# Decode attention over a K/V window: loading K and V one head at a time, or four heads at a time from one ring of buffers

## The chip, the cores and the metric

The kernel runs on one core of one Trainium2 chip. The metric is the device time of one execution in microseconds; lower is better. Engines are named as in the profile: PE is TensorE (matmuls), PEld its weight loads, ACT is ScalarE, DVE is VectorE, POOL is GpSimd, SP is SyncE, which issues nearly all DMAs (SPq is its queue).

## The reference

A decode step with one token for each of 8 sequences: layer norm, attention with 32 query heads and 8 K/V heads over the last 2048 cached positions, output projection and residual, then a small MLP block. The token-shift branch of that block is zero for one token, so only the following is left:

```python
B, D, Hq, Hkv, Sk, Dh, W = 8, 512, 32, 8, 8192, 128, 2048
q = (layernorm(x) @ wq)                          # [8, 32, 128]
k = k_cache[:, :, Sk - W:, :]                    # [8, 8, 2048, 128], each head serves 4 query heads
v = v_cache[:, :, Sk - W:, :]
p = softmax(q . k * Dh ** -0.5)                  # per sequence and query head, over 2048 positions
h = x + (p . v).reshape(8, 4096) @ wo
u = layernorm(h)
x1 = u
h2 = h + x1 + gelu(layernorm(x1) @ w3) @ w4      # w3 [512, 1792], w4 [1792, 512]
```

K and V of the window are 67.1 MB in bf16; wq and wo are 4.2 MB each, w3 and w4 1.8 MB each.

## The kernel before

**Prologue.** x is loaded and normalised, wq is loaded (32 KB per partition), and 128 matmuls (`pe_q`, L211) make q for all heads. `dve_q` puts the four queries of each K/V head at their place in `qblk`, a tile that POOL zeroed (L182), so that the 32 columns of one head's weights are zero except for its own four.

**Items.** The unit of work is one K/V head of one sequence (batch row): 64 items of 2048 positions. K of an item is one DMA of 512 KB into one of 11 slots of `knat`, 128 partitions with 16 positions (4 KB, one contiguous run) each. V is the same with 13 slots of `vnat`. For each item PE does:

- `pe_T` (L238): 16 transposes of 128x128 into PSUM, in two halves; `evict` copies the first half to SBUF on ACT (L246) and the second on DVE (L248).
- `pe_QK` (L256): four matmuls of 512 positions each in the four 32-column strips of the array. The eight items of a batch row accumulate into one score tile of 128x512: row 32q + h holds query head h over a quarter q of the positions.
- `pe_PV` (L313): 16 matmuls with V as weights and four columns of the transposed probabilities moving.

**Softmax of a batch row**, once for each eight items, is cut in five parts that lie between later items: the row maximum on DVE (`softmax_1`), its transpose and combination over the quarters (`softmax_2`), the negated maximum as a column and the exp of the whole 128x512 tile on ACT with its row sums (`softmax_3`, L282), four transposes of the probabilities and one copy to `pT_sb` (`softmax_4`, L291, L295), and the sum over the quarters and its reciprocal (`softmax_5`).

**Order.** One Python loop over steps p fixes the program order of every engine: in step p come the load of K for item p, its transposes and evictions, the softmax part that is due, QK for item p - 2 (`LQK`), and the load of V and PV for item p - 13 (`LV`). Each engine works through its own list in order and waits on semaphores; a wait holds back all that follows it in that list. SP's list has the loads in the order of the steps, wo in four parts at steps 15, 23, 31 and 39 (it reuses wq's buffer), and w3 and w4 at the end.

**End.** For the last batch row each head has its own PSUM area; after a head's PV comes its scaling by the reciprocal (`scale`) and the 16 matmuls of its four query heads with wo (`pe_wo`, L344). Then `hs` is copied (L409), and norm, w3, gelu, w4 and the store follow.

Of the kernel before, what the change touches and what calls it, by code (L numbers as in the profile page):

```python
# [6 lines left out]
dt = mybir.dt  # L7
# [4 lines left out]
B = 8  # L12
D = 512
H = 32
# [12 lines left out]
NK = 11  # L27
NV = 13
NKT = 4
LQK = 2  # L30
LV = 13
WO_AT = (15, 23, 31, 39)
# [32 lines left out]
def bass_sequential_preLN__sliding_block_cached__mixer_s_mlp__decode_kernel(  # L65
# [23 lines left out]
    with es:  # L89
# [27 lines left out]
        qblk = sb([128, B, G, H], dt.bfloat16, "qblk")  # L117
        knat = sb([128, NK, NC * DH], dt.bfloat16, "knat")
        vnat = sb([128, NV, NC * DH], dt.bfloat16, "vnat")
        kT_sb = sb([128, NKT, W], dt.bfloat16, "kT_sb")  # L120

        P_sb = sb([128, 2, 512], dt.bfloat16, "P_sb")
        pT_sb = sb([128, 2, NC, H], dt.bfloat16, "pT_sb")
# [27 lines left out]
        kT_ps = [ps_t([128, W], dt.bfloat16, f"kT_ps{i}") for i in range(2)]  # L151
# [9 lines left out]

        sem_k = [S(f"sem_k{i}") for i in range(NK)]
        sem_v = [S(f"sem_v{i}") for i in range(NV)]
# [4 lines left out]
        def dma(eng, dst, src, sem, *waits):  # L168
            def f(e):
# [12 lines left out]
        e_qz = PO.op(lambda e: e.memset(qblk[:], 0.0))  # L182
# [10 lines left out]
        e_sel = DV.op(lambda e: e.tensor_reduce(sel_f[:, :], ident_f[:, :].rearrange("p (q h) -> p h q", q=4),  # L193
                                                AX.X, ALU.add), e_idf)
# [11 lines left out]
        dma(SP, wq_v, A_wq.rearrange("(p k) n -> p k n", k=KC), sem_wq)  # L206

# [8 lines left out]
        def dve_q(e):  # L216
            for g in range(G):
                ins = e.tensor_scalar(qblk[:, :, g, R * g:R * (g + 1)],  # L218
                                      S_ps[0][:, R * g * B:R * (g + 1) * B].rearrange("p (i b) -> p b i", b=B),
                                      inv_sqrt_dh, None, ALU.mult)  # L220
            return ins
        e_qblk = DV.op(dve_q, e_q, e_qz)


        e_Tlo, e_Thi, e_lo, e_hi, e_QK, e_PV = {}, {}, {}, {}, {}, {}
        e_max, e_mT, e_neg, e_negps, e_negc, e_exp, e_PT, e_pT, e_lsel, e_Lb, e_rL, e_scale = ({} for _ in range(12))

        def K(i):
            return sem_k[i % NK], 16 * (i // NK + 1)

        def V(i):
            return sem_v[i % NV], 16 * (i // NV + 1)

        def pe_T(i):
            def half(lo):
                def f(e):
                    for c in range(lo, lo + NC // 2):
                        ins = e.matmul(kT_ps[i % 2][:, c * 128:(c + 1) * 128],  # L238
                                       knat[:, i % NK, c * DH:(c + 1) * DH], ident_b[:, :], is_transpose=True)
                    return ins  # L240
                return f
            e_Tlo[i] = PE.op(half(0), K(i), e_lo.get(i - 2), e_idb)
            e_Thi[i] = PE.op(half(NC // 2), e_hi.get(i - 2))

        def evict(i):
            e_lo[i] = AC.op(lambda e: e.activation(kT_sb[:, i % NKT, 0:W // 2], kT_ps[i % 2][:, 0:W // 2], ACT.Copy),  # L246
                            e_Tlo[i], e_QK.get(i - NKT))
            e_hi[i] = DV.op(lambda e: e.tensor_copy(kT_sb[:, i % NKT, W // 2:W], kT_ps[i % 2][:, W // 2:W]),  # L248
                            e_Thi[i], e_QK.get(i - NKT))

        def pe_QK(i):
            b, g = divmod(i, G)

            def f(e):
                for q in range(4):
                    ins = e.matmul(S_ps[b % 2][32 * q:32 * (q + 1), :], qblk[:, b, g, :],  # L256
                                   kT_sb[:, i % NKT, 512 * q:512 * (q + 1)],
                                   start=(g == 0), stop=(g == G - 1),
                                   tile_position=(0, 32 * q), skip_group_check=True)
                return ins  # L260
            e_QK[i] = PE.op(f, e_lo[i], e_hi[i], e_qblk, e_exp.get(b - 2))


        def softmax_1(b):
            e_max[b] = DV.op(lambda e: e.tensor_reduce(mcol[:, :], S_ps[b % 2][:, :], AX.X, ALU.max),  # L265
                             e_QK[G * b + G - 1], e_mT.get(b - 1))

        def softmax_2(b):
            e_mT[b] = PE.op(lambda e: e.matmul(sm[0:1, MROW], mcol[:, :], ident_f[:, :], start=True, stop=True),
                            e_max[b], e_rL.get(b - 1), e_idf)  # L270
            e = DV.op(lambda e: e.tensor_reduce(Mrow[:, :], sm[0:1, MROW].rearrange("o (q h) -> o h q", q=4),
                                                AX.X, ALU.max), e_mT[b])
            m_bc = bass.AP(tensor=Mrow[:, :].tensor, offset=0, ap=[[H, 1], [0, 4], [1, H]])
            e_neg[b] = DV.op(lambda e: e.tensor_scalar(negrow[:, :].rearrange("o (q h) -> o q h", q=4), m_bc,
                                                       -1.0, None, ALU.mult), e, e_negps.get(b - 1))

        def softmax_3(b):
# [4 lines left out]
            e_exp[b] = AC.op(lambda e: e.activation(P_sb[:, j, :], S_ps[j][:, :], ACT.Exp, bias=negcol[:, j:j + 1],  # L282
                                                    scale=1.0, accum_out=lcol[:, j:j + 1]),
                             e_negc[b], e_PT.get(b - 2), e_lsel.get(b - 2))

        def softmax_4(b):
            j = b % 2

            def f(e):
                for jt in range(4):  # L290
                    ins = e.matmul(pT_ps[:, jt * 128:(jt + 1) * 128], P_sb[:, j, 128 * jt:128 * (jt + 1)],  # L291
                                   ident_b[:, :], is_transpose=True)
                return ins
            e_PT[b] = PE.op(f, e_exp[b], e_negc[b])
            e_pT[b] = DV.op(lambda e: e.tensor_copy(  # L295
                pT_sb[:, j, :, :].rearrange("p (q jt) h -> p q jt h", jt=4),
                pT_ps[:, 0:NC * H].rearrange("p (jt q h) -> p q jt h", jt=4, q=4)),
                e_PT[b], e_PV.get(G * (b - 2) + G - 1))
            e_lsel[b] = DV.op(lambda e: e.tensor_scalar(lsel[:, :], sel_f[:, :], lcol[:, j:j + 1], None, ALU.mult),
                              e_Lb.get(b - 1), e_sel)  # L300

        def softmax_5(b):
            e_Lb[b] = PE.op(lambda e: e.matmul(sm[:, LB], ones_f[:, :], lsel[:, :], start=True, stop=True),
                            e_lsel[b], e_pT[b])
            e_rL[b] = DV.op(lambda e: e.reciprocal(rL[:, b % 2, :], sm[:, LB]), e_Lb[b],
                            e_scale.get(b - 2))

        def pe_PV(i, dst, *waits):
            b, g = divmod(i, G)

            def f(e):
                for c in range(NC):
                    ins = e.matmul(dst, vnat[:, i % NV, c * DH:(c + 1) * DH],  # L313
                                   pT_sb[:, b % 2, c, R * g:R * (g + 1)], start=(c == 0), stop=(c == NC - 1))
                return ins
            e_PV[i] = PE.op(f, V(i), e_pT[b], *waits)

        def scale(b, heads, src, *waits):
            return DV.op(lambda e: e.tensor_tensor(oT_all[:, heads, b], src, rL[:, b % 2, heads], ALU.mult),
                         e_rL[b], *waits)  # L320


        def load_k(i):
            dma(SP, knat[:, i % NK, :].rearrange("p (c d) -> p c d", c=NC),
                A_k_cache[i // G, i % G, W0:SK, :].rearrange("(p c) d -> p c d", c=NC), sem_k[i % NK],
                e_Thi.get(i - NK))

        def load_v(i):
            dma(SP, vnat[:, i % NV, :].rearrange("p (c d) -> p c d", c=NC),
                A_v_cache[i // G, i % G, W0:SK, :].rearrange("(p c) d -> p c d", c=NC), sem_v[i % NV],  # L330
                e_PV.get(i - NV))

        hT_ps = S_ps[0]
        e_sc7, e_wo = {}, []

        def pe_wo(g):
            def f(e):
                if g == 0:
# [3 lines left out]
                for h in range(R * g, R * (g + 1)):  # L342
# [4 lines left out]
            e_wo.append(PE.op(f, e_sc7[g], e_exp[NB - 2], e_scale[NB - 2], (sem_wo, 16 * len(WO_AT)), X))  # L347

        LAST = NB - 1
        E_LAST = G * LAST + G - 1 + LQK  # L350
        for p in range(NITEM + LV + 1):
            if p < NITEM:
                load_k(p)
                pe_T(p)
                evict(p)
            if p in WO_AT:
                n = WO_AT.index(p)
                hh = H // len(WO_AT)
                dma(SP, wo_v[:, n * hh:(n + 1) * hh, :],
                    A_wo[n * hh * DH:(n + 1) * hh * DH, :].rearrange("(h p) n -> p h n", p=DH), sem_wo, e_q)  # L360
            for b in range(NB):
                base = G * b + (G - 1) + LQK
# [4 lines left out]
                elif p == base + 3:  # L367
                    softmax_4(b)
                elif p == base + 4:
                    softmax_5(b)  # L370
            if 0 <= p - LQK < NITEM:
                pe_QK(p - LQK)
                b, g = divmod(p - LQK, G)
                if g == G - 1:
                    softmax_1(b)
            i = p - LV
            if 0 <= i < NITEM:
                load_v(i)
                b, g = divmod(i, G)
                heads = slice(R * g, R * (g + 1))  # L380
                if b < LAST:
                    pe_PV(i, oT_ps[:, heads], e_scale.get(b - 1))
                    if g == G - 1:
                        e_scale[b] = scale(b, slice(0, H), oT_ps[:, 0:H], e_PV[i])
                else:
                    dst = kbank[g % 4][:, 0:R]
                    pe_PV(i, dst, e_lo[NITEM - 1], e_hi[NITEM - 1], e_lo[NITEM - 2], e_hi[NITEM - 2],
                          e_sc7.get(g - 4))
                    e_sc7[g] = scale(b, heads, dst, e_PV[i])
# [125 lines left out]
```

## Time and profile before

| | us |
|---|---|
| median of 3 runs | 202.52 (202.40 to 202.85) |
| span of the profiled execution, first to last instruction | 200.5 |
| PE busy in it | 154.7 (77%) |
| ACT busy | 79.5 (40%) |
| DVE busy | 69.3 (35%) |
| K transposes on PE (L238), 1024 | 78.5 |
| K evictions on ACT (L246), 64 | 65.5 |
| exp on ACT (L282), 8 | 5.5 |
| DMA of the hardware queue | 79.18 MB, 97.7% of 16 engines' span |

The profile's times are from one execution's span, which leaves out what lies before the first and after the last instruction; the runs' times have that in them. Busy times of an engine are sums over stages that are limited by different things, and PE's clock varies (the mean granted clock was 0.839 of full speed), so the same matmul has more than one duration in the trace.

### The profile page before, as it was taken

To read this page: it belongs to the slowest core of one execution; us is meant where nothing else is said; L and a number is where in the kernel's file an instruction comes from. 1 tells how busy PE (TensorE), PEld (TensorE's weight loads), DVE (VectorE), ACT (ScalarE), POOL (GpSimd) and SP (SyncE) were. 2 spreads that over 40 slices of the span, in tenths; PEclk is the share of its full clock that TensorE was granted. 3 is DMA by queue.
4 is the path that set the end of the run, shared out by engine and by line. 5 is a ranking of instruction groups with operands and counts; after the bars stand their busy time and mean duration, and the time that the engine had idled before them with its cause. 6 is when DMAs were issued, how large, how long until landed. Compare 5 with 4: busy or idle time off the path is not lost.

```text
span 200.5 us, 6047 instructions
## 1 busy us (share of the span) xinstructions
PE 154.7 (77%) x2765; PEld 124.5 (62%) x2765; DVE 69.3 (35%) x165; ACT 79.5 (40%) x91; POOL 2.5 (1%) x10
## 2 busy tenths in 40 slices
PE   0039999798973998567883898878977869979685
PEld 0039777675862786356662776656765657669574
DVE  6103556434431344213341154324532343132122
ACT  6003778743541454423542255442644254240021
POOL 4000000000000000000000000000000000000000
PEclk9999999997999599958998599996999696555555
DMA  7989999999999999999999999999999999999950
GB/s 243 464 360 418 418 416 416 401 418 422 414 401 416 421 414 415 404 418 414 418 403 412 418 421 416 416 420 418 421 414 414 421 417 419 418 421 415 421 243 14
DMA packets 23641, 79.58 MB, mean 397 GB/s; under 512 B 2232, under 2 KB 6336, under 8 KB 23360
## 3 DMA queue, kind: packets, MB, share of 16 engines
q1 hardware_dynamic: 23600, 79.18, 97.7%
q8 instruction: 22, 0.36, 0.6%
q14 instruction: 3, 0.02, 0.0%
q10 hardware_dynamic: 16, 0.01, 0.0%
HBM read 79.18 MB, written 0.01 MB: 395 GB/s over the span
## 4 chain that ended last, share of the span: by engine, by line
DMA 75%; PE 20%; issue 2%; SPq 1%; DVE 1%
DMA knat<-in_A_k_cache_dram 61%; PE kT_ps L238 11%; DMA vnat<-in_A_v_cache_dram 7%; DMA wbig<-in_A_wq_dram 6%; PE S_ps L256 2%; PE S_ps L211 2%; PE kT_ps L428 2%; SPq L170 1%; PE S_ps L465 1%; PE oT_ps L313 1%; PE S_ps L344 1%; DVE kT_sb L248 0%; PE sm L411 0%; DVE mcol L265 0%; PE kT_ps L313 0%
## 5 line engine op out<-in xcount | busy, mean ns | idle before, releaser
L246 ACT ACTIVATE kT_sb<-kT_ps 128x1024 bf16<-128x1024 bf16 x64 | 65.5, 1023 | 94.8 <-PE kT_ps L238 94.7
L238 PE MATMUL kT_ps<-ident_b,knat 128*128 128x128 bf16 x1024 | 78.5, 239 | 17.0 <-DMA knat<-in_A_k_cache_dram 17.0
L238 PEld LDWEIGHTS kT_ps<-ident_b,knat 128*128 128x128 bf16 x1024 | 67.4, 108 | 22.4 <-DMA knat<-in_A_k_cache_dram 19.8
L248 DVE COPY kT_sb<-kT_ps 128x1024 bf16<-128x1024 bf16 x64 | 44.3, 691 | 96.2 <-PE kT_ps L238 96.1
L313 PEld LDWEIGHTS oT_ps<-pT_sb,vnat 128*128 128x128 bf16 x896 | 26.8, 98 | 24.0 <-DMA vnat<-in_A_v_cache_dram 12.5
L313 PE MATMUL oT_ps<-pT_sb,vnat 128*128 128x4 bf16 x896 | 31.6, 166 | 8.0 <-DMA vnat<-in_A_v_cache_dram 8.0
L256 PE MATMUL S_ps<-kT_sb,qblk 128*32 128x512 bf16 x256 | 30.0, 429 | 0.0
L256 PEld LDWEIGHTS S_ps<-kT_sb,qblk 128*32 128x32 bf16 x256 | 7.4, 95 | 5.4 <-issue 1.2
L211 PE MATMUL S_ps<-xlnT,wbig 128*128 128x8 bf16 x128 | 3.6, 168 | 7.9 <-DMA wbig<-in_A_wq_dram 7.9
L211 PEld LDWEIGHTS S_ps<-xlnT,wbig 128*128 128x128 bf16 x128 | 3.5, 104 | 7.9 <-issue 7.9
L282 ACT ACTIVATE P_sb<-S_ps,negcol 128x512 bf16<-128x512 f32 x8 | 5.5, 687 | 6.6 <-DVE negcol L281 6.6
L265 DVE TENSOR_REDUCE mcol<-S_ps 128x1 f32<-128x512 f32 x8 | 5.5, 681 | 2.0 <-PE S_ps L256 2.0
L344 PE MATMUL S_ps<-oT_all,wbig 128*128 128x8 bf16 x128 | 4.7, 168 | 1.6 <-issue 1.6
L440 ACT ACTIVATE s<-vsum,eps 128x8 f32<-128x8 f32 x1 | 0.3, 302 | 14.0 <-DVE vsum L437 14.0
L344 PEld LDWEIGHTS S_ps<-oT_all,wbig 128*128 128x128 bf16 x128 | 4.1, 104 | 1.8 <-issue 1.7
L313 PE MATMUL kT_ps<-pT_sb,vnat 128*128 128x4 bf16 x128 | 4.5, 167 | 0.5 <-DMA vnat<-in_A_v_cache_dram 0.5
L218 DVE TENSOR_SCALAR qblk<-S_ps 128x32 bf16<-128x32 f32 x8 | 0.9, 180 | 11.3 <-PE S_ps L211 11.3
L313 PEld LDWEIGHTS kT_ps<-pT_sb,vnat 128*128 128x128 bf16 x128 | 4.2, 106 | 0.7 <-DMA vnat<-in_A_v_cache_dram 0.7
L291 PE MATMUL sm<-ident_b,P_sb 128*128 128x128 bf16 x32 | 3.3, 230 | 1.7 <-ACT P_sb L282 1.7
L199 PE MATMUL sm<-ident_b,xln_b 8*128 8x8 bf16 x4 | 0.3, 175 | 5.1 <-DVE xln_b L191 5.1
L428 PEld LDWEIGHTS kT_ps<-uT,w_sb 128*128 128x128 bf16 x56 | 3.7, 161 | 0.8 <-DVE hc L415 0.8
L295 DVE COPY pT_sb<-sm 128x512 bf16<-128x512 bf16 x8 | 3.3, 416 | 2.3 <-PE sm L291 2.3
(67 smaller groups left out, 62.2 us busy)
## 6 DMA issues: line engine op xcount, KB each, us to landing
knat<-in_A_k_cache_dram SPq DMA_DIRECT2D x64, 512.0 KB, 14.7
vnat<-in_A_v_cache_dram SPq DMA_DIRECT2D x64, 512.0 KB, 15.0
wbig<-in_A_wq_dram SPq DMA_DIRECT2D x1, 4096.0 KB, 12.4
wbig<-in_A_wo_dram SPq DMA_DIRECT2D x4, 1024.0 KB, 16.3
w_sb<-in_B_w_dram SPq DMA_DIRECT2D x1, 1792.0 KB, 18.2
w_sb<-in_B_w_dram SPq DMA_DIRECT2D x1, 1280.0 KB, 20.3
w_sb<-in_B_w_dram SPq DMA_DIRECT2D x1, 512.0 KB, 16.8
x_sb<-in_A_x_dram ACTq DMA_DIRECT2D x1, 8.0 KB
```

What stands on the lines that cost most here:

```text
L211: ins = e.matmul(S_ps[0][:, h * B:(h + 1) * B], wq_v[:, kc, h * DH:(h + 1) * DH], xlnT[:, kc * B:(kc + 1) * B], start=(kc == 0), stop=(kc ...
L238: ins = e.matmul(kT_ps[i % 2][:, c * 128:(c + 1) * 128], knat[:, i % NK, c * DH:(c + 1) * DH], ident_b[:, :], is_transpose=True)
L246: e_lo[i] = AC.op(lambda e: e.activation(kT_sb[:, i % NKT, 0:W // 2], kT_ps[i % 2][:, 0:W // 2], ACT.Copy), e_Tlo[i], e_QK.get(i - NKT))
L248: e_hi[i] = DV.op(lambda e: e.tensor_copy(kT_sb[:, i % NKT, W // 2:W], kT_ps[i % 2][:, W // 2:W]), e_Thi[i], e_QK.get(i - NKT))
L256: ins = e.matmul(S_ps[b % 2][32 * q:32 * (q + 1), :], qblk[:, b, g, :], kT_sb[:, i % NKT, 512 * q:512 * (q + 1)], start=(g == 0), stop=(g ...
L265: e_max[b] = DV.op(lambda e: e.tensor_reduce(mcol[:, :], S_ps[b % 2][:, :], AX.X, ALU.max), e_QK[G * b + G - 1], e_mT.get(b - 1))
L282: e_exp[b] = AC.op(lambda e: e.activation(P_sb[:, j, :], S_ps[j][:, :], ACT.Exp, bias=negcol[:, j:j + 1], scale=1.0, accum_out=lcol[:, j:j ...
L291: ins = e.matmul(pT_ps[:, jt * 128:(jt + 1) * 128], P_sb[:, j, 128 * jt:128 * (jt + 1)], ident_b[:, :], is_transpose=True)
L295: e_pT[b] = DV.op(lambda e: e.tensor_copy(pT_sb[:, j, :, :].rearrange("p (q jt) h -> p q jt h", jt=4), pT_ps[:, 0:NC * H].rearrange("p (jt ...
L313: ins = e.matmul(dst, vnat[:, i % NV, c * DH:(c + 1) * DH], pT_sb[:, b % 2, c, R * g:R * (g + 1)], start=(c == 0), stop=(c == NC - 1))
L344: ins = e.matmul(hT_ps[:, nb * B:(nb + 1) * B], wo_v[:, h, nb * 128:(nb + 1) * 128], oT_all[:, h, :], start=False, stop=(h == H - 1), skip ...
L428: ins = e.matmul(y_ps[n][:, f * B:(f + 1) * B], w3_sb[:, kc, :].rearrange("p (f c) -> p c f", c=FC)[:, fc, :], uT[:, kc * B:(kc + 1) * B], ...
```

## The change

K and V go through one ring of six slots of 2 MB (`ring`). A load takes four heads of one batch row: partition 4p + h holds positions 64p to 64p + 63 of head h, one contiguous run of 16 KB. There are 32 such loads, issued by SP in the order K0, K1, wo, V0, K2, V1, K3, ...; two loads make a K or V of a batch row. A slot is free when the last transposes (K) or the last PV matmuls (V) that read it are done. The last V load is issued in four parts.

An item is now a quarter of the positions of four heads (`split`: batch row b, half j of the heads, quarter cq), so each 128-row chunk mixes four heads:

- QK takes for each head h every fourth column of the transposed K (`"p (x h) -> p h x"`) and accumulates the eight items of a batch row in the 32 score rows of strip h; the queries come from a window of `qwin` that puts them at column 8cq + 4j among zeros.
- exp is four instructions, one for each strip of 32 rows, and writes to every fourth column of `P_sb`, which POOL zeroed; the other heads' places stay zero.
- `P_sb` is four times as wide, so a batch row takes 16 transposes and four copies, in four steps.
- PV has 16 moving columns (four heads by four queries), of which the zeros cancel the wrong heads, and accumulates over 64 chunks.
- PV of item i comes in step i + 16 (`LPV`), one batch row behind the softmax; in the last batch row the output projection comes in two parts of 16 heads.

```diff
-NK = 11
-NV = 13
+NS = 6
 NKT = 4
+NCQ = W // 32
 LQK = 2
-LV = 13
-WO_AT = (15, 23, 31, 39)
+LPV = 16
...
+        qwin = sb([128, B, G, QW], dt.bfloat16, "qwin")
+        ring = sb([128, NS, NCQ * DH], dt.bfloat16, "ring")
+        P_sb = sb([128, 2, 512, 4], dt.bfloat16, "P_sb")
+        pT_sb = sb([128, 2, 16, 128], dt.bfloat16, "pT_sb")
...
+        e_pz = PO.op(lambda e: e.memset(P_sb[:], 0.0))
...
+        for b in range(NB + 1):
+            if b < NB:
+                loads += [("k", b, 0), ("k", b, 1)]
+            if b == 1:
+                loads += [("wo", n, 0) for n in range(4)]
+            if b >= 1:
+                loads += [("v", b - 1, 0), ("v", b - 1, 1)]
...
         def pe_QK(i):
...
+                for h in range(4):
+                    ins = e.matmul(S_ps[b % 2][32 * h:32 * (h + 1), :], qwin[:, b, 4 * j + h, w0:w0 + 32],
+                                   kT_sb[:, i % NKT, :].rearrange("p (x h) -> p h x", h=4)[:, h, :],
...
-            e_exp[b] = AC.op(lambda e: e.activation(P_sb[:, j, :], S_ps[j][:, :], ACT.Exp, bias=negcol[:, j:j + 1],
-                                                    scale=1.0, accum_out=lcol[:, j:j + 1]),
+            for h in range(4):
+                q = slice(32 * h, 32 * (h + 1))
+                e_exp[b] = AC.op(lambda e, h=h, q=q: e.activation(
+                    P_sb[q, j, :, h], S_ps[j][q, :], ACT.Exp, bias=negcol[q, j:j + 1], scale=1.0,
+                    accum_out=lcol[q, j:j + 1]),
...
+        def softmax_4(b, r):
...
+                for x in range(4):
+                    c = 4 * r + x
+                    ins = e.matmul(pT_ps[:, x * 128:(x + 1) * 128],
+                                   P_sb[:, j, 32 * c:32 * (c + 1), :].rearrange("p k h -> p (k h)"),
...
         def pe_PV(i, dst, *waits):
...
+                for c in range(16):
+                    n = 16 * cq + c
+                    ins = e.matmul(dst, ring[:, s, n * DH:(n + 1) * DH],
+                                   pT_sb[:, b % 2, c, :].rearrange("p (h c j r) -> p c j h r", h=4, c=4, j=2)[:, cq, j],
...
-        for p in range(NITEM + LV + 1):
-            if p < NITEM:
-                load_k(p)
+        for p in range(NG + LPV):
+            if p < NG:
                 pe_T(p)
                 evict(p)
...
+                elif base + 3 <= p <= base + 6:
+                    softmax_4(b, p - base - 3)
+            i = p - LPV
+            if 0 <= i < NG:
+                if i % 8 == 0:
                     softmax_5(b)
+                if (b, j) == (LAST, 1):
+                    dst = kbank[1][:, 0:16]
+                    pe_PV(i, dst, e_lo[NG - 1], e_hi[NG - 1], e_lo[NG - 2], e_hi[NG - 2])
...
+                elif (b, j) == (LAST, 1) and cq == 0:
+                    pe_wo(0)
...
+                elif (b, j) == (LAST, 1) and cq == 3:
+                    scale(b, 1, dst, e_PV[i])
+                    pe_wo(1)
...
+            src = (A_k_cache if what == "k" else A_v_cache)[b, 4 * j:4 * (j + 1), W0:SK, :].rearrange(
+                "h (p c) d -> p h (c d)", p=32)
+            free = taken[quads[n - NS]] if n >= NS else None
+            if l == LASTV:
+                for cq in range(4):
+                    cs = slice(16 * cq * DH, 16 * (cq + 1) * DH)
+                    dma(SP, ring[:, n % NS, cs], src[:, :, cs], sem_l[cq], free)
+            else:
+                dma(SP, ring[:, n % NS, :], src, sem_r[n % NS], free)
```

## The prediction

> **What bounds the kernel now.** I read the page first: its rows by slices, the queue, the chain.
>
> ```profile
> PE   0039999798973998567883898878977869979685
> PEclk9999999997999599958998599996999696555555
> DMA  7989999999999999999999999999999999999950
> ...
> q1 hardware_dynamic: 23600, 79.18, 97.7%
> ...
> DMA knat<-in_A_k_cache_dram 61%; PE kT_ps L238 11%; DMA vnat<-in_A_v_cache_dram 7%; DMA wbig<-in_A_wq_dram 6%; PE S_ps L256 2%; PE S_ps L211 2%; PE kT_ps L428 2%; SPq L170 1%; PE S_ps L465 1%; PE oT_ps L313 1%; PE S_ps L344 1%; DVE kT_sb L248 0%; PE sm L411 0%; DVE mcol L265 0%; PE kT_ps L313 0%
> ...
> L282 ACT ACTIVATE P_sb<-S_ps,negcol 128x512 bf16<-128x512 f32 x8 | 5.5, 687 | 6.6 <-DVE negcol L281 6.6
> ```
>
> The DMA row is full from slice 3 to the end: the stream of loads sets the end. TensorE (PE) is close behind, and its clock drops now and then. The windows view shows what precedes a drop (after the three instants: PE busy, time, and clock, DMA share, GB/s last):
>
> ```profile
> 43.89:47.31 3.42, 2.37 (x48) 1.84 (x45) 1.36 (x3) 1.02 (x1) 0.00 (x0) 0.99 1.01 408
> 47.31:50.72 3.41, 3.41 (x44) 2.53 (x42) 1.09 (x3) 1.02 (x1) 0.00 (x0) 0.51 1.05 426
> 60.96:64.37 3.41, 0.55 (x16) 0.47 (x16) 0.26 (x1) 0.14 (x1) 0.00 (x0) 0.99 1.03 417
> 64.37:67.79 3.42, 3.15 (x40) 2.52 (x41) 0.69 (x1) 1.02 (x1) 0.00 (x0) 0.50 1.03 422
> 67.79:71.20 3.41, 3.41 (x45) 2.77 (x43) 1.29 (x2) 1.02 (x1) 0.00 (x0) 0.51 1.03 418
> ```
>
> A stretch with a second or more of idle PE (2.37 of 3.42 us busy, 0.55 of 3.41) is followed by one or two stretches at half clock. Last, the chain in order of time near the end:
>
> ```profile
> 170.75 1.73 PE kT_ps L238 x16
> 172.47 0.55 PE S_ps L256 x4
> 173.02 0.53 PE oT_ps L313 x16
> 173.55 0.02 issue
> 173.57 14.08 DMA vnat<-in_A_v_cache_dram
> 187.65 0.05 issue
> 187.70 0.59 PE kT_ps L313 x16
> 188.29 0.05 PE S_ps L344 x2
> 188.34 1.39 issue
> 189.73 0.96 PE S_ps L344 x30
> 190.69 0.02 issue
> 190.71 0.20 DVE hs L409
> ```
>
> K is finished at 173; what remains is one V load per head, 0.59 us of PE behind each, and from `hs` a fixed 9.8 us to the span's end (200.5). The span lies 2.0 under the median of the runs (202.52), and I add that back.
>
> **The stream.** A 512 KB load is now 8 packets of 4 KB on each of 16 engines. The trace's packet records say 159 ns for 4 KB, 385 for 10 KB (w4), 1213 for 32 KB (wq, one every 1.21 us per engine). On that line a 16 KB packet takes 0.608 us; a 2 MB load, 8 of them per engine, takes 4.86 us, against 5.02 at the 418 GB/s of the stretches above. Over 32 loads the stream gains 5 us, if it never stops.
>
> **Does it stop?** A batch row is now 4 loads, 19.4 us. Six slots hold 1.5 rows. Load n waits for the readers of load n-6: the second K load of row b+1 waits for the last PV of row b-2, which PE issues in the last step of row b's transposes. SP issues in order, so V and all later loads queue behind that wait. PE's time x for the eight steps of a row therefore matters.
>
> One step at full clock: 16 transposes 1.00, QK 0.33 (four-matmul chain rows of 21 to 29 us), 16 PV matmuls 0.47; sum 1.80. At half clock 1.73 + 0.55 + 0.53 = 2.81. Eight full-clock steps: 14.4. Softmax on PE: 16 transposes of P where there were 4 (1.0), three small fp32 products (0.8): 16.2.
>
> **The exp.** One exp of 128x512 becomes four of 32x512. The row L282 gives 687 ns and its accumulator read starts 0.58 after it and takes 0.19: 0.79 for each pair, 3.2 for four, if the cost goes by elements per partition. No row has 32 partitions; the smallest ACTIVATE (128x8, 302 ns, the next 0.21 later) with its read would make 1.6 for four, and doubling for the 8-byte output step would make 5. I take 3.2, the row of the same length. The transposes of P come on PE after one more group of K transposes (1.0 us), as before; then PE waits: negcol is ready about 0.9 after the earlier group, so 0.9 + 3.2 - (negps 0.3 + PV 0.47 + QK 0.33 + transposes 1.0) = 2.0, with handovers 2.2 us a row. PV, QK and the next K transposes all queue behind that wait on PE, and one K eviction behind the exps on ACT (absorbed: its reader comes two steps later). So x = 18.4 at full clock.
>
> **The clock.** An idle 2.2 us in one stretch of 3.41 is the condition seen above. One half-clock stretch costs 3.41 x (1 - 1.80/2.81) = 1.2: x = 19.6. That leaves the ring no time: the release comes at x - 0.3, the next packet 1.05 after an issue (wq: issue 0.74, first packet 1.79), the landing 0.5 later, so a row whose load is late takes x + 1.3 = 20.9; a late load gives the next row slack, which then goes at the stream's 19.4, or 19.8 with the slowest engine's lag (in the landing records the last of 16 engines trails the first by 0.8 us for wq, 1.8 at 20 us, 4.4 at 165). The middle is a row period R = 20.4.
>
> **Costed at little.** QK reads K^T with a step of 8 bytes. Nearest rows: weight loads with that step (L199, 115 ns) against 104 packed, and L428 (28-byte step, 161) against 104: from nothing to +55% of 0.33, up to 1.5 us a row; I take nothing, as L199 is nearer. The Trainium skill (SBUF — State Buffer, Door 1: The DMA port swizzle) says that two hits in each 16-byte line keep full bandwidth; 8-byte steps give two, so by it the sum stands, and by L428's row it would be 8 us more. PV with 16 columns for 4: the 8-column matmuls of L211 start 28 ns apart, PV's 30; nothing, at most 12 columns of 0.49 ns (0.8 us a row). POOL's larger zeroing (1.80 us for 2048 columns, so 7 for 3840 + 4096) ends by 10 us, before wq lands at 13.2; uncovered it would delay the first QK. Three more copies of 0.42 a row on DVE (35% busy) run beside PE.
>
> **The end.** K2's first load lands at 13.2 (wq) + 19.4 (K0, K1) + 11.4 (wo, 256 packets of 46 ns per engine, at the observed overlap) + 14.6 (V0 and it) + 1.0 (slow engine) = 60 us; PE has long been idle then (its first two rows end near 41). Rows 2 to 6: 5R = 102. Row 7: x = 19.6. Then a tail that PE alone makes, at the half clock of the rows above: two QK and two PV 2.2, the maximum and its transpose with one PV 1.6, negps and PV 0.9, four exps beyond that PV 2.9, four P transposes with four PV 3.8, denominator 0.5, five PV of row 7 2.6, output projection of 16 heads 2.05 (64 matmuls; 30 took 0.96), three PV 1.6, scaling 0.3, second half of the projection 2.05: 20.5. Then 9.8. Sum 60 + 102 + 19.6 + 20.5 + 9.8 = 211.9; with 2.0, **213.9**. The last V is not in it: its slot is freed at the end of row 7's steps and it lands 6 us later, its first use 14 later; w3 and w4, queued behind it on SP (8.6 us at 418 GB/s), land some 15 later, their first use 22. Before, PE finished K 15 us ahead of the last V; now K comes two V pairs ahead, but in 2 MB lumps, and P's path stands behind it.
>
> **Rivals.**
> Full clock kept: R = 19.8, x = 18.4: 60 + 99 + 18.4 + 30.3 (tail and 9.8) = 207.7, **209.7**. For it: 50 to 61 us stayed full with short waits; against: the two stretches above.
> QK slowed by its step, or exp by its output step: x and R up by 1.5 to 2.6: 60 + 112 to 115 + 22 + 30.5, **226 to 230**.
> Faster: the stream sets the end as now. If four exps cost a fourth each and hide under the next K transposes, and the slow engine's lag vanishes: 59 + 5 x 19.4 + 16.2 + 16.1 (full-clock tail without the exp wait) + 9.8 = 198.1, **200.1**. It decides where x and tail together fall from 40.1 to under 33.7 at R = 19.4. Against it is L282: its time does not look like one that shrinks with partitions, though no row says so.
> No gain in the packets (2 MB at 418 GB/s): 60.8 + 103 + 19.6 + 30.3 = 213.7, **215.7**.
> Slow source: each load now reads four heads 2 MB apart at once. wq's first packets, when all engines started together, took 1.87 us on average against 1.21; at that pace a load takes 7.5, and 13.2 + 32 x 7.5 + 11.4 + 13 + 2 = **280**. [...]
>
> **Numbers.** Forecast 0.52, full clock 0.19, slowed reads or writes 0.11, faster 0.08, no packet gain 0.06, slow source 0.04. Low end 204: the forecast with exps at 1.6 (x and tail 3 less, R at 19.8); high end 224, short of the worst of the slowed reads. What a measurement can tell from no change is 0.2%, 0.4 us: faster 0.08, same 0.02, slower 0.90.
>
> **What would show it.** In the profile after: 16 KB packets near 0.61 us; stops in the DMA row from 75 us on; four exps of 0.6 to 0.7 us and PE waiting 2 us per row for P; K rows starting 20 to 21 us apart; the last PV near 200 with V landed long before. Wrong if the DMA row stays full and the chain still ends in V, or if packets exceed 0.7 us.

## The result and the profile after

The changed kernel takes **236.16 us** (median of 4 runs, 235.71 to 236.84) against 202.49 for the kernel before on the same chip: 1.1664 times as long, 95% interval 1.1642 to 1.1685. The sign was forecast, the size was not: 213.9, with a range that ended at 224. The profiled execution spans 234.4 us. Below, medians are over all runs of a kernel and ratios over its fast runs; the profiled run of qk_packed (235.0 us) and one run of spread were slow, and from the former only durations of single instructions are read.

From the page of the changed kernel (rows by slices, queue, chain by engine and by line, two groups):

```profile
PE   0069995480892999299939992999299929817985
PEclk9999999587599799779976997699859988955555
DMA  7999999999999249995998599849995999699100
...
q1 hardware_dynamic: 10208, 79.18, 82.3%
...
PE 53%; ACT 19%; DMA 13%; SPq 10%; DVE 3%; issue 1%
PE kT_ps L261 21%; ACT P_sb L310 17%; PE S_ps L281 10%; SPq L170 10%; PE oT_ps L346 8%; DMA ring<-in_A_k_cache_dram 8%; DMA wbig<-in_A_wq_dram 5%; PE sm L321 5%; ACT kT_sb L270 2%; PE S_ps L370 2%; PE S_ps L213 2%; PE kT_ps L469 1%; PE sm L334 1%; PE sm L294 1%; DVE pT_sb L326 1%
...
L310 ACT ACTIVATE P_sb<-S_ps,negcol 32x512 bf16<-32x512 f32 x32 | 44.4, 1388 | 7.6 <-DVE negcol L307 6.9
...
L281 PE MATMUL S_ps<-kT_sb,qwin 128*32 128x512 bf16 x256 | 40.1, 612 | 0.0
```

The DMA row, full before, now falls to 2 to 6 about once a batch row from slice 14 on. PE's row falls to 1 to 3 one or two slices ahead of each of these falls: PE stops first, for something else than the stream, and then the stream waits for the slots that PE frees late. The chain says for what PE stops. Loads made 74% of it (K, V and wq); now K and wq make 13%, and the exps, L310, make 17%. One exp of 32x512 takes 1388 ns; the one of 128x512 before, with four times the elements, took 687. The view of waits gives the total (us, times, longest):

```profile
PE sm L321 <- ACT P_sb L310: 36.3, 8, 5.8
```

and the chain in order of time (start, us, what) shows one such wait, in row 2's softmax:

```profile
92.25 0.16 DVE negcol L307
92.41 0.02 issue
92.44 1.40 ACT P_sb L310 x2
...
96.70 1.40 ACT P_sb L310 x2
98.10 0.05 issue
98.14 0.61 PE sm L321 x4
```

Four exps with their reads (two more of 1.39 us at 93.87 and 95.28) follow one another for 5.65 us, and PE's next transposes of P start 0.05 after the last. Behind such a wait the clock falls, as before: in the stretch from 187.70 to 191.20 PE is busy for 0.36 us, and in the next 3.40 us its clock is 0.59.

Against the sum of the prediction, from the same trace:

| term | forecast | measured |
|---|---|---|
| row 2's first transposes | 60 | 59.3 |
| five rows, 2 to 6 | 102 (20.4 each) | 118.9 (23.8 each) |
| row 7's eight steps | 19.6 | 22.7 |
| tail to `hs` | 20.5 | 23.8 |
| `hs` to the end | 9.8 | 9.7 |
| span | 211.9 | 234.4 |

The 22.5 us lie in the rows (16.9), in row 7 (3.1) and in the tail (3.3), where PE sets the pace.

### The profile page after: what moved, and what is told of

It is laid out like the page before. It is cut to its first block, busy times and chain, and to the rows that moved or that the text cites. A ratio compares the mean times of both kernels' runs of the same rounds, so it can differ in the third digit from the quotient of the medians.

```text
span 234.4 us, 6181 instructions
## 1 busy us (share of the span) xinstructions
PE 171.2 (73%) x2861; PEld 133.7 (57%) x2861; DVE 81.4 (35%) x191; ACT 118.0 (50%) x139; POOL 7.6 (3%) x11
## 4 chain that ended last, share of the span: by engine, by line
PE 53%; ACT 19%; DMA 13%; SPq 10%; DVE 3%; issue 1%
PE kT_ps L261 21%; ACT P_sb L310 17%; PE S_ps L281 10%; SPq L170 10%; PE oT_ps L346 8%; DMA ring<-in_A_k_cache_dram 8%; DMA wbig<-in_A_wq_dram 5%; PE sm L321 5%; ACT kT_sb L270 2%; PE S_ps L370 2%; PE S_ps L213 2%; PE kT_ps L469 1%; PE sm L334 1%; PE sm L294 1%; DVE pT_sb L326 1%
## 5 line engine op out<-in xcount | busy, mean ns | idle before, releaser
L261 PEld LDWEIGHTS kT_ps<-ident_b,ring 128*128 128x128 bf16 x1024 | 67.3, 108 | 36.3 <-issue 17.5
L261 PE MATMUL kT_ps<-ident_b,ring 128*128 128x128 bf16 x1024 | 78.6, 239 | 8.6 <-DMA ring<-in_A_k_cache_dram 8.6
L310 ACT ACTIVATE P_sb<-S_ps,negcol 32x512 bf16<-32x512 f32 x32 | 44.4, 1388 | 7.6 <-DVE negcol L307 6.9
L321 PE MATMUL sm<-ident_b,P_sb 128*128 128x128 bf16 x128 | 16.1, 265 | 36.6 <-ACT P_sb L310 36.3
L281 PE MATMUL S_ps<-kT_sb,qwin 128*32 128x512 bf16 x256 | 40.1, 612 | 0.0
L346 PE MATMUL oT_ps<-pT_sb,ring 128*128 128x16 bf16 x960 | 33.9, 172 | 0.0
L346 PEld LDWEIGHTS oT_ps<-pT_sb,ring 128*128 128x128 bf16 x960 | 32.1, 101 | 2.1 <-issue 2.0
L321 PEld LDWEIGHTS sm<-ident_b,P_sb 128*128 128x128 bf16 x128 | 10.5, 118 | 38.2 <-ACT P_sb L310 37.6
L326 DVE COPY pT_sb<-sm 128x512 bf16<-128x512 bf16 x32 | 13.4, 418 | 38.6 <-PE sm L321 38.6
L310 ACT ACTIVATION_READ_ACCUMULATOR P_sb<-S_ps,negcol 32x1 f32 x32 | 8.0, 249 | 0.0
## 6 DMA issues: line engine op xcount, KB each, us to landing
wbig<-in_A_wo_dram SPq DMA_DIRECT2D x4, 1024.0 KB, 16.9
```

The lines of the kernel that those rows point to most:

```text
L261: ins = e.matmul(kT_ps[i % 2][:, c * 128:(c + 1) * 128], ring[:, s, n * DH:(n + 1) * DH], ident_b[:, :], is_transpose=True)
L281: ins = e.matmul(S_ps[b % 2][32 * h:32 * (h + 1), :], qwin[:, b, 4 * j + h, w0:w0 + 32], kT_sb[:, i % NKT, :].rearrange("p (x h) -> p h x" ...
L310: e_exp[b] = AC.op(lambda e, h=h, q=q: e.activation(P_sb[q, j, :, h], S_ps[j][q, :], ACT.Exp, bias=negcol[q, j:j + 1], scale=1.0, accum_ou ...
L321: ins = e.matmul(pT_ps[:, x * 128:(x + 1) * 128], P_sb[:, j, 32 * c:32 * (c + 1), :].rearrange("p k h -> p (k h)"), ident_b[:, :], is_tran ...
L326: e_pT[b, r] = DV.op(lambda e: e.tensor_copy(pT_sb[:, j, 4 * r:4 * (r + 1), :].rearrange("p c n -> p (c n)"), pT_ps[:, :]), e_PT[b, r], e_ ...
L346: ins = e.matmul(dst, ring[:, s, n * DH:(n + 1) * DH], pT_sb[:, b % 2, c, :].rearrange("p (h c j r) -> p c j h r", h=4, c=4, j=2)[:, cq, j ...
```

## Experiments

Two things were open. Is it the exps' output step (8 bytes), their number of partitions, QK's read step (8 bytes), or the ring? And what is each worth alone? The theory at the outset was that both steps cost and that the ring adds what its late K loads make. The table has the runs in the order in which they are told; rows are means of rows 2 to 6, waits are PE's, from each run's profiled execution.

| kernel | median us | row 2 starts | row | last K transpose starts | wait for P | wait for K |
|---|---|---|---|---|---|---|
| changed | 236.16 | 59.3 | 23.8 | 199.7 | 36.3 | 8.6 |
| qk_packed | 231.74 | | | | | |
| exp_flat | 223.07 | 59.2 | 22.4 | 189.1 | 16.4 | 16.6 |
| both_flat | 222.18 | 59.4 | 21.6 | 185.6 | 16.9 | 21.8 |
| runs4 | 232.59 | 56.3 | 23.6 | 196.3 | 36.3 | 6.1 |
| order | 228.80 | 52.4 | 23.5 | 192.0 | 36.3 | 1.2 |
| both_flat_order | 206.87 | 49.6 | 20.5 | 171.2 | 17.9 | 3.0 |
| exp_flat_order | 208.77 | 50.5 | 20.7 | 173.2 | 16.4 | 1.2 |
| spread | 210.97 | 59.5 | 20.3 | 177.5 | 4.7 | 28.8 |
| spread_order | 204.47 | 49.5 | 20.4 | 170.9 | 4.7 | 5.1 |
| best | 200.02 | 49.4 | 20.1 | 163.1 | 4.7 | 4.4 |
| best_runs4 | 202.87 | 46.8 | 20.6 | 162.8 | 4.8 | 1.6 |

**qk_packed: QK's operand packed.** The transposes use an identity with its columns permuted, so that the four heads' positions come out as four runs.

```diff
+        e_perm = DV.op(lambda e: e.tensor_copy(perm_b[:, :].rearrange("m (h p) -> m p h", h=4),
+                                               ident_b[:, :].rearrange("m (p h) -> m p h", h=4)), e_idb)
...
-                                       ring[:, s, n * DH:(n + 1) * DH], ident_b[:, :], is_transpose=True)
+                                       ring[:, s, n * DH:(n + 1) * DH], perm_b[:, :], is_transpose=True)
...
-                                   kT_sb[:, i % NKT, :].rearrange("p (x h) -> p h x", h=4)[:, h, :],
+                                   kT_sb[:, i % NKT, :].rearrange("p (c h k) -> p h c k", c=16, h=4)[:, h],
```

> K's transposes use a column-permuted identity, so that each head's columns of the transposed K stand in runs of 32 and QK reads packed; all else is the changed kernel. Theory (PE's path sets the end, and the 8-byte steps are what the forecast sized wrongly): the four QK matmuls take 0.33 us at full clock instead of 0.55, 8 x 0.22 = 1.8 us a row over some six rows, so about 226 us, and the DMA row still stops. Rival (the ring and its stops set the end): QK gets shorter, PE waits longer for loads, 235 to 236.

Measured: 231.74 us (1.1429, 1.1378 to 1.148). By the ratios that is a gain of 4.8 us, known to about 1, where 10 was expected. The step does slow the matmuls; from its page:

```profile
L284 PE MATMUL S_ps<-kT_sb,qwin 128*32 128x512 bf16 x256 | 28.7, 436 | 0.0
```

By the start times in the traces, a group of four packed matmuls takes 0.33 us at full clock and 0.55 at half; with the step of 8 bytes it takes 0.55 to 0.57 at either. So packing shortens the groups, but only where the clock is full, and the rows then stop at P and K as before.

**exp_flat: the exps write packed.** Each strip's 512 results go to a run of their own in `P_sb`, still four instructions of 32 partitions. The probabilities then stand in the wrong places, so only the time means anything.

```diff
-                    P_sb[q, j, :, h], S_ps[j][q, :], ACT.Exp, bias=negcol[q, j:j + 1], scale=1.0,
+                    P_sb[q, j, 128 * h:128 * (h + 1), :].rearrange("p k h -> p (k h)"), S_ps[j][q, :], ACT.Exp, bias=negcol[q, j:j + 1], scale=1.0,
```

> The four exps write the same number of values packed instead of to every fourth column, so the probabilities lie in the wrong places; only the time is read. Theory (the 8-byte output step costs ACT twice the time): 32x512 packed takes about 0.69 us and 0.79 from one to the next instead of 1.41; PE's wait for P falls from 4.2 to about 1.8 us a row, seven waits, so about 219 us. Rival (32 partitions in four instructions cost that much by themselves): 1.39 us each and 236 us. Rival (ring): shorter exps, but 233 or more.

Measured: 223.07 us (1.1025, 1.1005 to 1.1046), 13.1 less. The group and the wait that answer to the changed kernel's:

```profile
L310 ACT ACTIVATE P_sb<-S_ps,negcol 32x512 bf16<-32x512 f32 x32 | 21.7, 678 | 7.4 <-DVE negcol L307 6.8
```

```profile
PE sm L321 <- ACT P_sb L310: 16.4, 8, 3.3
```

With packed writes an exp of 32x512 takes 678 ns, as the one of 128x512 did (687), and PE waits 16.4 us for P in eight rows instead of 36.3. The fall of 19.9 is eight times the 2.5 us by which the four exps with their reads became shorter (5.66 to 3.16 in one row of each trace). The median won only 13.1 of it: the wait for K rose from 8.6 to 16.6.

**probe: the step by itself.** ACTIVATEs of 512 columns of exp ahead of q's matmuls in the changed kernel, all reading PSUM, with the number of partitions and the output step varied (and groups like QK's with read steps of 2, 4 and 8 bytes).

```diff
...
+            e_pr = AC.op(lambda e: e.activation(pr_o4(32, 1), S_ps[1][0:32, :], ACT.Exp), e_pr)
+            e_pr = AC.op(lambda e: e.activation(pr_o4(32, 2), S_ps[1][0:32, :], ACT.Exp), e_pr)
+            e_pr = AC.op(lambda e: e.activation(pr_o4(32, 4), S_ps[1][0:32, :], ACT.Exp), e_pr)
+            e_pr = AC.op(lambda e: e.activation(pr_o4(32, 8), S_ps[1][0:32, :], ACT.Exp), e_pr)
+            e_pr = e_pra = AC.op(lambda e: e.activation(pr_o4(128, 4), S_ps[1][:, :], ACT.Exp), e_pr)
```

> The changed kernel with extra instructions while PE and ACT wait for wq: groups of four QK-shaped matmuls that read a zero tile with steps of 2, 4 and 8 bytes, and exps of 512 columns on 128 and on 32 partitions with output steps of 2, 4, 8 and 16 bytes. Theory (the step is the cost): matmuls of about 0.39, 0.39 to 0.61 and 0.61 us; exps 0.6 to 0.7 us on 32 as on 128 partitions when packed, 1.2 to 1.4 with 8 bytes on 128 partitions too. Rival (the number of partitions is the cost): 32 partitions packed take 1.2 us or more.

The groups by line, in the order of the diff (steps of 2, 4, 8 and 16 bytes on 32 partitions, then 8 bytes on 128):

```profile
L229 ACT ACTIVATE kT_sb<-S_ps 32x512 bf16<-32x512 f32 x2 | 1.2, 587 | 0.1
L230 ACT ACTIVATE kT_sb<-S_ps 32x512 bf16<-32x512 f32 x2 | 1.5, 730 | 0.1
L231 ACT ACTIVATE kT_sb<-S_ps 32x512 bf16<-32x512 f32 x2 | 2.6, 1296 | 0.1
L232 ACT ACTIVATE kT_sb<-S_ps 32x512 bf16<-32x512 f32 x2 | 4.9, 2430 | 0.1
L233 ACT ACTIVATE kT_sb<-S_ps 128x512 bf16<-128x512 f32 x2 | 2.6, 1304 | 0.1
```

128 partitions packed took 597 ns. So the number of partitions changes next to nothing (587 against 597, 1296 against 1304), and the output step sets the time from 4 bytes on. The TensorE half told little: back to back on zeros, groups with steps of 2, 4 and 8 bytes started 0.40, 0.43 and 0.46 us apart, unlike the 0.33 and 0.55 within the kernels. Why they differ is open.

**both_flat: both together.** The edits of the two runs above.

> The packed QK reads and the packed exp writes together (the probabilities lie in the wrong places; only the time is read). These are the two prices that the forecast had assumed, so theory (only those two terms were sized wrongly) gives the forecast's own number, 213.9 us, with PE waiting 2.2 us a row for P and rows of 20.4 us. Rival (a further cost that the forecast lacks, in the ring's waits or PE's clock): rows of 21.5 us or more and 220 us.

Measured: 222.18 us (1.0949, 1.0901 to 1.0997): the rival held. With PE's own work as the forecast had it, rows last 20.8, 23.6, 20.8, 23.2 and 19.7 us: every other row finds its K late. The load order became the question.

**runs4: four DMAs for each load.** The path by which K reaches PE, without touching PE: each 2 MB load is four DMAs, in runs of 4 KB, with their own semaphores, so that PE may start on the first quarter.

```diff
...
+            for cq in range(4):
+                cs = slice(16 * cq * DH, 16 * (cq + 1) * DH)
+                dma(SP, ring[:, n % NS, cs], src[:, :, cs], sem_r[n % NS][cq], free)
```

> Every 2 MB load is issued as four DMAs of 512 KB in 4 KB runs (a quarter of the positions of the same four heads), each with its own semaphore; slots, order and all work are those of the changed kernel. Theory (PE's path sets the end): packets of 0.159 us and a stream of 418 instead of 431 GB/s change nothing from row to row; only the first row that waits for its load (59 us) starts up to 3.6 us earlier, as a quarter is enough to begin, less 0.8 for the slower stream: 233 us. Rival (the stream sets the end): 4% more time per load in 100 us of stream, 240 us.

Measured: 232.59 us (1.1486, 1.1461 to 1.151). Row 2 starts 3.0 us sooner, about as expected, and the rest stays: rows 23.6, wait for P 36.3.

**order: loads interleaved by halves.** The changed kernel with one edit: V stands two rows behind K in SP's list, and K's and V's halves alternate (K2a, V0a, K2b, V0b, ...).

```diff
-        for b in range(NB + 1):
-            if b < NB:
-                loads += [("k", b, 0), ("k", b, 1)]
-            if b == 1:
+        for b in range(NB + 2):
+            if b == 2:
                 loads += [("wo", n, 0) for n in range(4)]
-            if b >= 1:
-                loads += [("v", b - 1, 0), ("v", b - 1, 1)]
+            for j in range(2):
+                if b < NB:
+                    loads += [("k", b, j)]
+                if b >= 2:
+                    loads += [("v", b - 2, j)]
```

> The changed kernel with only the order of the loads altered: V of row b-2 is interleaved half by half with K of row b (K0, K1, wo, then K2 first half, V0 first half, K2 second half, V0 second half, ...), so that a K half and the V half of the same steps land together and both slots come free together; no load waits for PV of a later step. Theory (PE's path sets the end, the ring adds about 1 us a row): rows go at PE's own 22.7 instead of 23.8, and row 2 starts 9.7 us earlier as two loads less stand ahead of it: 236.2 - 9.7 - 5.5 = 221 us, with the DMA queue waiting for slots. Rival (the ring's stops are the main loss): rows near 20 us and 207 us or less.

Measured: 228.80 us (1.1317, 1.1278 to 1.1357): 7.4 less, of which row 2's earlier start is 6.9. Neither number held: 221 had row 2 9.7 us earlier and rows of 22.7, and 207 had rows near 20. PE hardly waits for K any more (1.2 us in all), and rows still last 23.5. So in the changed kernel the rows are PE's own, and the ring hides behind them; in both_flat the ring was uncovered.

**both_flat_order and exp_flat_order: each step alone, with short waits for K.** The edits of both_flat, and of exp_flat, on top of order.

> The kernel of the run both_flat (packed QK operand; the four exps write packed, so the probabilities stand in the wrong places) with the loads of K and V interleaved by halves, V two rows behind K. It asks why both_flat's rows stayed at 21.6 us, 20.8 and 23.6 by turns. Theory: K loads that come late, since the ring's slots are released in the bursts of four steps of the changed kernel's load order (PE waited 21.8 us for K there, 11.0 before row 2): with the order changed the waits for K go, rows are 20.3 us and the median is 206 to 208 us. Rival: the rows are PE's own at the granted clock, then they stay at 21.6 us and the earlier start of row 2 alone counts, 7 us: 215 us.

> The run both_flat_order with QK reading K^T in steps of 8 bytes again: the four exps write packed (the probabilities stand in the wrong places), the loads are interleaved by halves. Between this run and order lies the exps' output step alone, between this run and both_flat_order QK's read step alone, and in none of the three does PE wait for K to speak of. Theory: a QK group takes 0.55 us instead of 0.33 at full clock and the same 0.55 at half clock (in the changed kernel's records the groups are 0.551 to 0.572 whatever the clock, in the kernels with the packed operand 0.33 or 0.55), so with a fifth of the groups at half clock it costs 0.22 x 64 x 0.8 = 11 us over 64 groups: 218 us, and the exps' step the other 11 of the 22 us between order and both_flat_order. Rival: QK's longer groups fill time in which PE would wait for P or V anyway; then this is 207 to 211 us and the exps' step costs nearly all.

Measured: both_flat_order 206.87 us (1.0219, 1.0205 to 1.0232), as the theory had it, rows 20.5. exp_flat_order 208.77 us (1.0305, 1.0282 to 1.0329): its theory fell, its rival held. Of the 21.9 us between order and both_flat_order, taken off in this order, the exps' output step makes 20.0 and QK's read step 1.9. Where the rest of QK's step went shows in the clock, in the chain by engine and in the waits for V, first of exp_flat_order, then of both_flat_order:

```profile
PEclk9999999958789999999979997999799979955555
...
PE 57%; DMA 13%; ACT 13%; SPq 11%; DVE 4%; issue 2%
...
PE oT_ps L347 <- DMA ring<-in_A_v_cache_dram: 2.7, 1, 2.7
```

```profile
PEclk9999999759679799979967996999699969555555
...
PE 41%; DMA 35%; SPq 11%; ACT 7%; DVE 3%; issue 2%
...
PE oT_ps L350 <- DMA ring<-in_A_v_cache_dram: 5.0, 4, 3.6
```

With the packed operand QK's busy time falls by 11.7 us (39.9 to 28.2). PE's whole busy time falls by 8.1 only (167.3 to 159.2): its clock is lower (0.881 to 0.836), so its other matmuls take longer. The span falls by 1.2 (206.1 to 204.9): the other 6.9 us are idle time, most of it longer waits for V (2.7 to 5.0 us), K (1.2 to 3.0) and P (16.4 to 17.9). Loads now make 35% of the chain where they made 13%. So this is what the rival named, QK's longer groups filling time in which PE would wait anyway, and the clock takes the smaller part. The 1.9 us are what the step costs beside a stream that nearly sets the pace, and not its price where PE alone does.

**spread and spread_order: the cheap way to the same tile.** One packed exp of 128x512 as before; DVE then writes each quarter of the positions among zeros, by a mask of four columns, ahead of the transposes that need it. QK's operand is packed. spread has the changed kernel's load order, spread_order the interleaved one.

```diff
+            e_exp[b] = AC.op(lambda e: e.activation(E_sb[:, j, :], S_ps[j][:, :], ACT.Exp, bias=negcol[:, j:j + 1],
+                                                    scale=1.0, accum_out=lcol[:, j:j + 1]),
...
+        def spread_P(b, r):
...
+            e_spr[b, r] = DV.op(lambda e: e.tensor_tensor(P_sb[:, j, 128 * r:128 * (r + 1), :], src4, own_bc, ALU.mult),
```

> Packed QK reads by the permuted identity, and the softmax mended: one exp of 128x512 as in the kernel before, packed, and four multiplications on DVE of 128x512 by a 0/1 mask, one ahead of each group of P transposes, that spread the values among zeros. Order of loads as in the changed kernel. Theory: PE's wait for P falls from 4.2 us to under 0.5 a row, x is about 17 us, rows go at the stream's 19.4 to 19.8 (late loads now and then), tail 18: 59.5 + 99 + 17.5 + 18 + 9.8 + 1.8 = 205.6 us. Rival (the ring's wait, x + 1.3, and the clock stay): rows of 21 us, 212 us.

> The mended softmax and QK and the interleaved order of loads together. Theory: no load waits for a slot, the stream runs full to the end (13.2 + 11.4 + 32 x 4.86 = 180, the last V 2 to 3 us later with the slowest engine), PE is done with all but the last PV by then: 183 + 0.6 + 0.3 + 2.05 + 9.8 + 1.8 = 197.5 us, 2.5% under the kernel before. Rival (PE's path still sets the end: row 2 at 50, rows of 20, tail 18): 50 + 120 + 18 + 9.8 + 1.8 = 199.6 or more.

Measured: 210.97 us (1.0385, 1.0332 to 1.0438) and 204.47 us (1.0087, 1.0057 to 1.0118). The wait for P falls to 4.7 us in eight, since PE now waits for one exp and one spread (685 ns) at most; 32 spreads cost DVE 21.8 us beside PE. Both theories missed: spread came out near its rival's 212, and spread_order within its rival's "199.6 or more". In spread the wait for K took back much of what the wait for P gave (it rose from 8.6 to 28.8 us, 13.5 of them ahead of row 2); in spread_order the last V lands at 183.7, 4 us before the kernel before, and `hs` comes at 193.3: PE is late by its own order, with V5's PV ahead of K7's last transposes.

**best and best_runs4: another end, and the size of the packets.** best is spread_order with K7 loaded ahead of V5, V6 and V7, and PE's list in its last 24 steps put in that order; best_runs4 is best with runs of 4 KB in four DMAs for each load. That also lets PE start on a quarter, so the two differ in more than the packets.

```diff
+            if p < NG:
+                if p < 56:
+                    pv_item(p - LPV)
+            elif p >= 68:
+                pv_item(p - LPV - 4)
...
+            if 64 <= p < 68:
+                pv_item(40 + 2 * (p - 64))
+                pv_item(41 + 2 * (p - 64))
```

> The kernel of the run spread_order (packed QK operand, one packed exp, VectorE spreads the quarters by a 0/1 mask, loads of K and V interleaved by halves with V two rows behind K) with another end: K7's halves are loaded ahead of V5, V6 and V7, and PE's queue does row 7's transposes and QK with no PV among them; V5's PV comes two items a step behind them, and V6's and V7's one a step later by four. Theory: in spread_order the end was PE's own order, T63 waiting behind PV items whose V5b landed at 163.9 though K7b had landed at 157.8, and PE was 10 us behind the stream. With that removed the stream sets the end again: last V at 183.7, then 0.6 + 0.3 + 1.9 to hs at 186.6, + 9.7 + 1.8 outside: 198 us, below the kernel before (202.5). Rival: row 7's softmax and 24 PV items behind it still end after the stream, hs at 192 or later, and no less than 203 us.

> The same as the run best, but each 2 MB load is four DMAs of 4 KB runs (256 bytes of 16 positions), each with a semaphore of its own. Theory (the forecast's stream term): where the stream sets the end, 16 KB runs are worth 4.86 against 5.02 us for each of 32 loads, 5 us in all, so this is 203 us, some 5 us above best, with the last V 4 to 5 us later. Rival: the runs4 run of the changed kernel won 3.6 us by its first quarter coming early; if that counts here and the packets do not, it is 195 to 198 us.

Measured: best **200.02 us** (199.89 to 200.34; 0.9882, 0.9866 to 0.9897), 1.2% under the kernel before; best_runs4 202.87 us (1.0015, 1.0006 to 1.0023). Best's DMA row, and the last part of its chain in order of time:

```profile
DMA  6999999999999999999999999999999999999930
```

```profile
155.75 23.01 DMA ring<-in_A_v_cache_dram
...
178.81 1.88 PE oT_ps L367 x64
...
181.35 1.80 PE S_ps L391 x64
183.15 0.30 PE kT_ps L367 x11
183.45 1.73 issue
```

The stream is full to its end and sets the time again. The 2.0 us over the theory's 198 lie behind the last V: `hs` is at 188.5 and not 186.6, after 1.73 us in which PE waits for nothing that the profile shows (the kernel before has 1.39 of the same kind there). The traces' packet records show what goes with it. The queue that the page calls instruction (q8) has a packet of 16 KB under way when PE stops, from 183.00 to 183.96 in best and from 187.45 to 188.41 in the kernel before; PE goes on 1.2 and 1.3 us behind the packet's end. The pauses marked issue near the end of spread, spread_order, both_flat_order and exp_flat_order also end 1.3 to 1.5 us behind such a packet. That PE waits there for its own program is a reading of these times and not shown by a run.

## Why the prediction was wrong

**Where it held.** The sign, and the reason for it: the release of slots and the path through P replace the stream as the bound. The packets: 611 ns for 16 KB, forecast 608. The loads, with four heads 2 MB apart at once, ran at 428 to 436 GB/s in slices 8 to 12 of the page, where the row is full, so the slow source is out. The Trainium skill (DMA: Bandwidth & Descriptors, Latency and other measured facts) gives copies between HBM tensors with a row pitch of 2 MiB 164 GB/s per direction, where a padded pitch reaches 214; the loads here go to SBUF, and these slices show no such loss. The stream's term, 5 us: the last V of best lands 4.5 us before that of best_runs4 (183.7 against 188.2), and 2.85 of it reaches the end. Row 2 at 60 (59.3). PV with 16 columns at nothing (172 ns each, a group 0.49 against 0.47). The PE path of a row, nearly: with exps at 0.79 a pair, as the forecast had them, PE waits 1.69 us for P in six of the eight rows and 2.05 on the mean (forecast 2.2), and the rows of exp_flat_order last 20.7 with 1.2 us of waiting for K in all; x was 19.6.

**The step that failed: the exp.** The text bounded four exps by 1.6 and 5, named the doubling for the 8-byte output step as the upper end, and took 3.2, "the row of the same length". Measured: 4 x 1.41 = 5.65, above even that end. The end itself was short: with the text's own 0.58 doubled and 0.19 for the read of the accumulator, four pairs make 4 x (1.16 + 0.19) = 5.4 and not 5, and the read takes 0.25 us instead of 0.19 besides. That the cost goes by elements per partition was right (probe: 32 and 128 partitions alike); that it does not go by the step was the error. The Trainium skill (ScalarE: Activation LUTs, What ACT_TABLE_LOAD costs) gives one element per cycle for every function, by which 280 + 0.833 x 512 makes an estimate of 0.71 us. Packed, the trace agrees (0.68); with a step of 8 bytes it is 1.39, so here that rule holds for packed output alone. The 2.45 us too little per row, eight times over, are 19.6 us: 20.0 between order and exp_flat_order, 13.1 in the changed kernel's own order, where the ring takes 7 of them back.

**The second step: the ring's row.** With exps at the forecast's price, exp_flat still takes 223.1, 9.2 above the forecast. Its rows are 22.4, where the text took 20.4 as the middle between a late row (20.9) and one at the stream's pace. Rows 4, 5, 6 and 7 start after 2.2, 0.3, 2.3 and 1.1 us of PE waiting for K, and rows of 21.9 and 22.7 show no row in which the slack of a late load is used up at the stream's pace. With the loads interleaved by halves (exp_flat_order) these waits are all but gone, rows are 20.7, row 2 starts 8.7 us sooner and the last K transpose ends 15.9 us sooner; the medians differ by 14.3. Which release makes which load late, by how much, was not followed load by load.

**QK's read step, taken at nothing,** cost 1.9 us of 207 beside a nearly full stream, and about 4.8 in the changed kernel's order. The first number is near nothing by luck: the text took the step to be free for PE. The Trainium skill (SBUF — State Buffer, Door 1: The DMA port swizzle) has two hits in each 16-byte line at full bandwidth; the traces differ: with two hits a line QK's group took 0.55 us instead of 0.33 at full clock, and the exp's writes 1.30 instead of 0.59. QK's loss in the end was small because packed groups left PE waiting longer for V, K and P and at a lower clock, as the two kernels above show; the text had no such term.

**The clock.** The text read that a stretch with "a second" (a microsecond is meant) or more of idle PE is followed by stretches at half clock. The same view of the kernel before has two stretches with 1.12 and 1.02 us idle (33.65 to 37.07 and 91.68 to 95.09) whose next one kept 1.00, and no such exception from 1.23 us idle on. The term of one half-clock stretch in a row rests on 2.2 us and is not touched.

**The rivals.** "QK slowed by its step, or exp by its output step" (226 to 230, 0.11) was the mechanism, sized too small: it raised a row by 1.5 to 2.6 over 20.4, and rows rose by 3.4. Two ends of the text do not come out of its own terms: 1.5 more a row makes five rows 109.5 and not 112, so this rival begins near 224; and exps at 1.6 take some 1.6 us each off row 7 and the tail, which with R at 19.8 gives about 208 and not 204. The row L282 had been read for its length in elements; no row of before had a strided write on ACT, and the bound for it deserved more than a tenth.

## What to carry to other kernels

Price an instruction's access pattern on each side by itself: a row of the same shape says nothing on a strided write, and four instructions that each take twice as long stand in the path in full once another engine waits for the last of them. Writing among zeros is cheap where it is pipelined by quarters on an idle engine (DVE, 0.68 us each, 0.6 us of waiting a row) and dear on the one that the chain goes through. Large packets pay where the stream sets the end: in best, loads in runs of 16 KB are worth 2.85 us against four loads in runs of 4 KB, and in the changed kernel, where PE sets the end, the four small loads were 3.6 us faster, as PE could start on the first.

## What was not expected of the hardware

- An ACTIVATE of 512 columns takes 0.59 us with an output step of 2 bytes, 0.73 with 4, 1.30 with 8 and 2.43 with 16: about proportional to the step from 8 bytes on. With 2 and 8 bytes 128 partitions took the same as 32.
- Within these kernels QK's groups of four matmuls with a moving operand in steps of 8 bytes take 0.55 us whatever the granted clock; packed, 0.33 at full and 0.55 at half clock. At half clock the step is free. Groups on zeros in the probe did not show it as clearly (0.46 against 0.40).
- A kernel with longer matmuls and shorter waits on PE was granted the higher clock (0.881 against 0.836) and lost only 1.9 us for 8 more us of busy time.
- Pauses of PE that no semaphore explains (0.57 to 1.96 us near the end of six kernels) ended 1.2 to 1.5 us behind a 16 KB packet of the instruction queue.
